# Linear attention and gated feed-forward: banks, order and sums of the attention's first pairs

## The chip, the cores and the metric

The kernel runs on one core of a Trainium2 chip, in one launch. Its time is the device time in microseconds; the median of three runs counts. The core's engines are TensorE (PE in the profile, with its weight loads as PEld), VectorE (DVE), ScalarE (ACT), GpSimd (POOL) and SyncE (SP), which issues all DMAs here. Each engine works off its own instructions strictly in the order of the program, and semaphores make it wait for the others.

## What is computed

First an attention with feature maps, for 8 batches and 8 heads of 576 x 64; its output, 4608 tokens of 512 features, then goes through a gated feed-forward layer.

```python
def phi(x):
    proj = np.einsum('bhsd,df->bhsf', x, w_phi)
    proj = proj - np.max(np.abs(proj), axis=-1, keepdims=True)
    return np.concatenate([np.exp(proj), np.exp(-proj)], axis=-1)
q_p, k_p = (phi(q), phi(k))
kv = np.einsum('bhsf,bhsd->bhfd', k_p, v)
z = np.sum(k_p, axis=2)
num = np.einsum('bhsf,bhfd->bhsd', q_p, kv)
den = np.einsum('bhsf,bhf->bhs', q_p, z)[..., None] + 1e-06
x = (num / den)                       # to (4608, 512)
gate = 1.0 / (1.0 + np.exp(-(x @ w_gate)))
out = gate * (x @ w_val) @ w_out      # d_model 512, d_ff 1536
```

## The kernel before

The attention works on pairs of heads: 32 steps, numbered 0 to 31, four to a batch (NP = 4). A pair i passes through these steps, each a function of the listing:

- `load`, `load_v`: K, Q and V from DRAM into buffers of which there are two each.
- `keys` and `rest`: the projections of K on TensorE, in three parts (`pk_0`, `pk_1` in `k_heads`, `pk_2` in `rest`). `k_exp` then takes the maximum (`mx`, L432) and the difference (`dk`, L445) on VectorE, and both exponentials (`ek`, L454) on ScalarE. From pair EARLY on, `k_sum` adds up four blocks of the exponentials per head on VectorE (`s2`, `su`, L467 and L468).
- `q_half`: a half of Q's projection on TensorE for each head (`pq`, L411); `copies` brings it to `d` on ScalarE (L473). `q_max` finds the maximum over the features on VectorE (L500 to L513: a transposing reduction `pm`, small copies to `pn`, a transpose to `mb`) and subtracts it from `d` (L518). `q_exp` makes both exponentials on ScalarE, `eq0` and `eq1` (L564), into one buffer each; `d` has two buffers.
- `kv`: the products of the key exponentials with V, and their sums over the sequence by products with ones (`kvz`, L528 and L542): five blocks per head, or two where `k_sum` has added four. `turn` transposes the result (`tp`, L554); ScalarE copies before and behind it (`kvt`, `kv`).
- `num`: numerators `nm` (L580) and denominators `dp` (L591) on TensorE, copied by ScalarE to `ex` (L597) and `dr` (L607). `norm` brings the denominators through DRAM to every row (three DMAs: `dn`, `den`, `rb`), takes the reciprocal, and `scale` multiplies (`xp`, L634) and stores x. For the last pair of the first batch (`soon=True`) the denominators are computed for every row instead, without the DMAs. In the first batch `scale` also splits x into `xh` and `xl` in place, for the feed-forward's first chunks.

PSUM is cut into pools: `ps_gv` (two banks, gate and value products), `ps_a` (five banks, everything of the attention, through the helper `bank`), and `ps_acc` (one bank, output products).

While the attention runs, `half_units` gives the work of the feed-forward's first four blocks of d_ff on chunks of 256 tokens: half units of twelve gate or value products (`gv`, L164), the gating on ScalarE and VectorE (`gate`), and outputs of twelve products (`acc`, L171). `fill` puts half units between the attention's steps at a given rate; `queue` makes a batch's chunks due LAG spots later. `weigh` makes the twelve weight tiles of these blocks (`weight_tile`: three cheap and two longer VectorE instructions and one of ScalarE, L133 to L143) as far as `grant` allows. Generators in `tasks` go on by one step at each `tick`; where a tick stands sets where their instructions come in the engines' queues. The rest of the feed-forward (L171 and L164 on tiles of 512 tokens) follows from about 700 us on.

The order is written by hand: one loop for pairs -1 to EARLY - 1 = 3 (L728 to L752), then `num` of pair 3 with `soon`, then one loop from pair EARLY - 1 on (L756 to L784) with `fill` in it.

Of the kernel before, what the change touches and what calls it, by code (L numbers as in the profile page):

```python
# [20 lines left out]
F = 128  # L21
# [15 lines left out]
EARLY = NP  # L37
RATE = 2.8
LAG = (2, 8)
# [5 lines left out]
def attention_moe(  # L45
# [306 lines left out]
    with ExitStack() as actx:  # L352
# [9 lines left out]
        def bank(shape, name):  # L362
            return ps_a.tile(shape, F32, tag="a", name=name)
# [14 lines left out]
        steps = [(b, p) for b in range(B) for p in range(NP)]  # L378
# [23 lines left out]
        def q_half(i, hf):  # L402

            n = f"{i}_{hf}"
            if hf == 0:
                ds[i] = at.tile([P, 2, S], F32, tag="d", name=f"d{i}")
            x, d = loaded["q", i], ds[i]
            cs = slice(hf * HS, hf * HS + HS)
            pps = [bank([P, HS], f"pq{n}{hd}") for hd in range(2)]
            for hd in range(2):  # L410
                nc.tensor.matmul(  # L411
                    pps[hd], wk[head(hd), :], x[head(hd), cs], start=True, stop=True
                )
            return [(d[:, hd, cs], pps[hd]) for hd in range(2)]
# [64 lines left out]
        def rest(i):  # L479
            kx = loaded.pop(("k", i))  # L480
            pp = bank([P, 4, F], f"pk{i}_2")
            nc.tensor.matmul(pp[:, 0, :], kx[:, 4 * P :], wk, start=True, stop=True)  # L482
# [37 lines left out]
        def kv(i):  # L520
# [3 lines left out]
            kvz = bank([P, 3 * F], f"kvz{i}")  # L524
# [25 lines left out]
        def turn(i):  # L550
            kvt = kvs[i]
            tp = bank([P, 3, P], f"tp{i}")
# [5 lines left out]
        def q_exp(i):  # L558
            yield
            d = ds.pop(i)  # L560
            es = []
            for sg in range(2):
                e = at.tile([P, 2, S], F32, tag=f"eq{sg}", name=f"eq{i}_{sg}", bufs=1)
                act.activation(e, d, AF.Exp, scale=1.0 - 2.0 * sg)  # L564
                es.append(e)
                yield
            exps[i] = es

        def num(i, soon=False):
# [4 lines left out]
            nms = [bank([P, HS], f"nm{i}_{hf}") for hf in range(2)]  # L574
            dps = [bank([P, HS], f"dp{i}_{hf}") for hf in range(1 + soon)]
            for hf in range(2):
                cs = slice(hf * HS, hf * HS + HS)
                for sg in range(2):
                    for o in range(0, P, Q):
# [4 lines left out]
                        )  # L584
            for n, dp in enumerate(dps):
# [10 lines left out]
            for hf in range(2):  # L596
                act.copy(ex[:, hf * HS : hf * HS + HS], nms[hf])  # L597
# [12 lines left out]
        def norm(i, ex, dr):  # L610
# [4 lines left out]
            for _ in range(3):  # L615
                yield
# [10 lines left out]
            for _ in range(4):  # L627
                yield
            yield from scale(i, ex, rb)

        def scale(i, ex, rb):
# [3 lines left out]
            for c in range(S // CH if b == 0 else 0):  # L635
# [3 lines left out]
                ps = slice(p * CH, p * CH + CH)  # L639
                split(xs[c][0][:, ps], xs[c][1][:, ps], xp[:, c * CH : c * CH + CH])  # L640
                parts[c] += 1
            yield
# [79 lines left out]
        N = len(steps)  # L722
# [5 lines left out]
        for i in range(-1, EARLY):  # L728
            load(i + 2 if i >= 0 else N)
            if i + 1 < EARLY:  # L730
                keys(i + 1)
                copies(q_half(i + 1, 0))
                tick()
                tick()
                copies(q_half(i + 1, 1))
                rest(i + 1)
                start(q_max(i + 1))
                tick()
# [11 lines left out]
            tick()  # L750
            tick()
            grant(i)  # L752
        num(EARLY - 1, True)
        grant(6)
        queue(0)
        for i in range(EARLY - 1, N + 1):  # L756
            if EARLY <= i:
                load(i + 2)
                grant(3 * (i - 1))
# [8 lines left out]
            if i < EARLY:  # L768
                fill()
                fill()  # L770
                continue
# [94 lines left out]
```

## Time and profile before

| | us |
|---|---|
| three runs | 1295.61, 1295.95, 1300.03 |
| median | 1295.95 |
| the profiled execution | 1297.41 |
| its span, first to last instruction | 1295.6 |
| TensorE busy in it | 1228.6 (95%) |
| VectorE busy | 797.9 (62%) |
| ScalarE busy | 526.8 (41%) |
| mean granted TensorE clock | 0.97 |

The page's slices cut the span into 40 equal parts of 32 us; a digit is the busy share in tenths, and PEclk the granted TensorE clock in tenths:

```profile
PE   7848899999999999999889999999999999999998
DVE  6699888788878778883894953424343434333333
PEclk8967899999999999999899999999999999999999
```

Engines overlap, so busy shares do not add up to the span; a stage is read by the engine that is full in it and by what the others wait for.

### The profile page before, as it was taken

What the parts mean: (1) busy time and instruction counts of PE and PEld (TensorE: products, weight loads), DVE (VectorE), ACT (ScalarE), POOL (GpSimd) and SP (SyncE); (2) the same over time, 40 slices, a digit from 0 to 9 for tenths busy, and PEclk for the clock granted to TensorE, in tenths of its full rate; (3) what the DMA queues carried; (4) which work ended last, traced back from release to release, by engine and by line L of the source; (5) the groups of instructions that cost most, each with busy time, mean ns of one, the idle gap of its engine ahead of it and who ended that gap; (6) DMA issues with size and microseconds to landing.
All of it is one profiled execution on the core that took longest, in us unless ns stands there. A gap on an engine that the chain in (4) does not pass through costs nothing.

```text
span 1295.6 us, 22470 instructions
## 1 busy us (share of the span) xinstructions
PE 1228.6 (95%) x9120; PEld 970.1 (75%) x9120; DVE 797.9 (62%) x1608; ACT 526.8 (41%) x1081; POOL 0.7 (0%) x6
## 2 busy tenths in 40 slices
PE   7848899999999999999889999999999999999998
PEld 5535566777777777777778888888888888888886
DVE  6699888788878778883894953424343434333333
ACT  4535556665565566564443422222222222222221
POOL 0000000000000000000000000000000000000000
PEclk8967899999999999999899999999999999999999
DMA  4556344343343334332763620202011111111010
GB/s 175 178 178 243 105 124 136 98 137 97 124 127 111 110 104 126 105 109 72 264 209 133 209 98 1 83 15 71 28 58 40 57 42 46 52 39 60 5 61 33
DMA packets 80868, 131.55 MB, mean 102 GB/s; under 512 B 18300, under 2 KB 37884, under 8 KB 80764
## 3 DMA queue, kind: packets, MB, share of 16 engines
q1 hardware_dynamic: 80764, 130.11, 30.9%
q8 instruction: 72, 1.18, 0.4%
q14 instruction: 32, 0.26, 0.1%
HBM read 92.04 MB, written 28.45 MB: 93 GB/s over the span
## 4 chain that ended last, share of the span: by engine, by line
PE 81%; DVE 11%; ACT 3%; issue 2%; DMA 2%; SPq 0%; DVEq 0%; ACTq 0%
PE acc L171 21%; PE g L164 15%; PE v L164 15%; PE gv L164 12%; PE kvz L528 5%; PE nm L580 4%; PE pq L411 2%; PE dp L591 2%; PE pk L421 2%; ACT eq L564 1%; PE kvz L542 1%; DMA wraw<-w_moe 1%; PE pk L482 1%; DVE mb L513 1%; PE tp L554 1%
## 5 line engine op out<-in xcount | busy, mean ns | idle before, releaser
L164 PE MATMUL gv<-xh,wh 128*128 128x256 f32 x576 | 174.5, 303 | 17.0 <-ACT xh L62 11.9
L171 PE MATMUL acc<-wh,hh 128*128 128x512 f32 x432 | 172.4, 399 | 3.4 <-ACT hh L234 2.7
L164 PE MATMUL gv<-xl,wh 128*128 128x256 f32 x576 | 167.2, 290 | 2.8 <-DVE xl L211 2.8
L171 PE MATMUL acc<-wh,hl 128*128 128x512 f32 x432 | 169.2, 392 | 0.7 <-DVE hl L236 0.7
L171 PE MATMUL acc<-wl,hh 128*128 128x512 f32 x432 | 169.1, 392 | 0.0
L164 PE MATMUL gv<-xh,wl 128*128 128x256 f32 x576 | 166.5, 289 | 0.0
L164 PEld LDWEIGHTS gv<-xh,wh 128*128 128x128 f32 x576 | 114.1, 198 | 34.6 <-issue 14.9
L62 ACT CAST hh<-u 128x512 fp32r<-128x512 f32 x72 | 44.7, 621 | 229.4 <-DVE u L185 229.4
L183 DVE TENSOR_SCALAR t<-t 128x512 uint32<-128x512 uint32 x72 | 30.7, 426 | 167.2 <-ACT t L180 167.2
L164 PEld LDWEIGHTS gv<-xl,wh 128*128 128x128 f32 x576 | 114.1, 198 | 3.9 <-DVE xl L211 3.0
L180 ACT ACTIVATE t<-g 128x512 f32<-128x512 f32 x72 | 43.0, 598 | 179.5 <-PE g L164 179.3
L164 PEld LDWEIGHTS gv<-xh,wl 128*128 128x128 f32 x576 | 114.0, 198 | 0.0
L164 PE MATMUL g<-xh,wh 128*128 128x512 f32 x288 | 113.0, 392 | 0.0
L164 PE MATMUL v<-xh,wh 128*128 128x512 f32 x288 | 112.6, 391 | 0.0
L164 PE MATMUL g<-xh,wl 128*128 128x512 f32 x288 | 112.5, 391 | 0.0
L164 PE MATMUL g<-xl,wh 128*128 128x512 f32 x288 | 112.5, 391 | 0.0
L164 PE MATMUL v<-xl,wh 128*128 128x512 f32 x288 | 112.3, 390 | 0.0
L164 PE MATMUL v<-xh,wl 128*128 128x512 f32 x288 | 112.1, 389 | 0.0
L184 DVE SCALAR_TENSOR_TENSOR t<-t,v 128x512 f32<-128x512 f32 x72 | 49.4, 686 | 97.7 <-PE v L164 97.7
L171 PEld LDWEIGHTS acc<-wh,hh 128*128 128x128 f32 x432 | 81.1, 188 | 26.2 <-issue 4.8
L171 PEld LDWEIGHTS acc<-wh,hl 128*128 128x128 f32 x432 | 81.2, 188 | 20.2 <-DVE hl L236 1.7
L171 PEld LDWEIGHTS acc<-wl,hh 128*128 128x128 f32 x432 | 81.3, 188 | 15.8
(92 smaller groups left out, 2120.5 us busy)
## 6 DMA issues: line engine op xcount, KB each, us to landing
wraw<-w_moe SPq DMA_DIRECT2D x36, 512.0 KB, 4.6
xl<-xs SPq DMA_DIRECT2D x34, 512.0 KB, 3.9
k<-k SPq DMA_DIRECT2D x32, 320.0 KB, 3.7
v<-v SPq DMA_DIRECT2D x32, 320.0 KB, 2.9
q<-q SPq DMA_DIRECT2D x32, 288.0 KB, 4.1
wh<-wtop SPq DMA_DIRECT2D x36, 256.0 KB, 2.3
ys<-y SPq DMA_DIRECT2D x36, 256.0 KB, 2.0
yp<-ys SPq DMA_DIRECT2D x36, 256.0 KB
```

The costliest lines, as they stand in the source:

```text
L62: a = act.copy(h, x)
L164: nc.tensor.matmul(o, a[:, ws], x[:, cs], start=i == 0, stop=i == 11)
L171: nc.tensor.matmul(acc, a[:, ts], w[:, ws], start=first and i == 0, stop=last and i == 2)
L180: act.activation(t, g, AF.Tanh, scale=0.5)
L183: vec.tensor_scalar(tu, tu, 0x7FFFFFFF, None, op0=ALU.bitwise_and)
L184: vec.scalar_tensor_tensor(t, t, 1.0, vl, op0=ALU.add, op1=ALU.mult)
L411: nc.tensor.matmul(pps[hd], wk[head(hd), :], x[head(hd), cs], start=True, stop=True)
L421: nc.tensor.matmul(pps[hd][:, t, :], kx[head(hd), t * P : t * P + P], wk[head(hd), :], start=True, stop=True,)
L482: nc.tensor.matmul(pp[:, 0, :], kx[:, 4 * P :], wk, start=True, stop=True)
L528: nc.tensor.matmul(kvz[o : o + Q, : 2 * F], vx[:, 2 * t + hd, o % D : o % D + Q], (e0, e1)[hd][:, t, :] if t < 4 else e2[:, 0, :], start=t ...
L580: nc.tensor.matmul(nms[hf][o : o + Q, :], w[:, sg, o : o + Q], es[sg][:, o // D, cs], start=sg == 0, stop=sg == 1, tile_position=(0, o),)
L591: nc.tensor.matmul(dp[o : o + Q, :], w[:, 2, z : z + Q], es[sg][:, hd, hf * HS : hf * HS + HS], start=sg == 0, stop=sg == 1, tile_position ...
```

## The change

Six things change in the first 200 us:

- In the first batch (pairs 0 to 3) the KV products and their transposes use the output bank (`ps_acc`), numerators and denominators the two gate and value banks (`ps_gv`), since the feed-forward has not begun. `bank` chooses by the pair's number. `ps_a` then holds only the projections.
- `num` copies the numerators to `ex` ahead of the denominators' products (which then need only the bank of the first).
- Q's second exponential is written over `d`, which gets a third buffer; the first has two buffers under one name (`eq`).
- The sums of the keys stay on TensorE up to pair 9 (ONPE = 10), where VectorE added up blocks from pair 4 on: pairs 4 to 9 get twelve more products with ones and lose four VectorE additions each.
- The order in the first batch is written anew: `rest` (`pk_2`) comes behind `kv`, the `norm` of the first batch waits fewer ticks, and pair 4 is projected in the loop's last round, ahead of pair 3's numerators. `scale` makes all copies `xh`, then yields, then all differences `xl`.
- The feed-forward's queue starts behind that loop, with LAG 4 instead of 2 (the old second loop began one round earlier), and the weight tiles 3 to 5 are granted only there.

```diff
+ONPE = 10
-LAG = (2, 8)
+LAG = (4, 8)
...
-        def bank(shape, name):
+        def bank(shape, name, i=N, ps=None, tag=None):
+
+            if i < EARLY:
+                return ps.tile(shape, F32, tag=tag, name=name)
             return ps_a.tile(shape, F32, tag="a", name=name)
...
-                ds[i] = at.tile([P, 2, S], F32, tag="d", name=f"d{i}")
+                ds[i] = at.tile([P, 2, S], F32, tag="d", name=f"d{i}", bufs=3)
...
-                if i >= EARLY:
+                if i >= ONPE:
                     yield
                     yield from k_sum(i)
...
-            kvz = bank([P, 3 * F], f"kvz{i}")
+            kvz = bank([P, 3 * F], f"kvz{i}", i, ps_acc, "acc")
...
-            tp = bank([P, 3, P], f"tp{i}")
+            tp = bank([P, 3, P], f"tp{i}", i, ps_acc, "acc")
...
-            es = []
-            for sg in range(2):
-                e = at.tile([P, 2, S], F32, tag=f"eq{sg}", name=f"eq{i}_{sg}", bufs=1)
-                act.activation(e, d, AF.Exp, scale=1.0 - 2.0 * sg)
-                es.append(e)
-                yield
-            exps[i] = es
+            e = at.tile([P, 2, S], F32, tag="eq", name=f"eq{i}")
+            act.activation(e, d, AF.Exp)
+            yield
+            act.activation(d, d, AF.Exp, scale=-1.0)
+            exps[i] = e, d
+            yield
...
-            nms = [bank([P, HS], f"nm{i}_{hf}") for hf in range(2)]
-            dps = [bank([P, HS], f"dp{i}_{hf}") for hf in range(1 + soon)]
+            nms = [bank([P, HS], f"nm{i}_{hf}", i, ps_gv, "gv") for hf in range(2)]
             for hf in range(2):
...
+                act.copy(ex[:, cs], nms[hf])
+            dps = [bank([P, HS], f"dp{i}_{hf}", i, ps_gv, "gv") for hf in range(1 + soon)]
...
-            for _ in range(3):
+            for _ in range(3 if i >= EARLY else 2):
                 yield
...
-            for _ in range(4):
+            for _ in range(4 if i >= EARLY else 2):
                 yield
...
         for i in range(-1, EARLY):
             load(i + 2 if i >= 0 else N)
...
+            if i == EARLY - 1:
+                start(q_exp(i))
+            keys(i + 1)
+            copies(q_half(i + 1, 0))
+            copies(q_half(i + 1, 1))
+            if i == EARLY - 1:
                 tick()
             if i >= 0:
                 kv(i)
-                start(q_exp(i))
+            tick()
+            rest(i + 1)
             if i >= 1:
                 num(i - 1)
             tick()
+            start(q_max(i + 1))
+            if 0 <= i < EARLY - 1:
+                start(q_exp(i))
             tick()
             if i >= 0:
                 turn(i)
                 load_v(i + 2)
-            tick()
-            tick()
+            if i == EARLY - 1:
+                num(i, True)
+            for _ in range(3):
+                tick()
             grant(i)
-        num(EARLY - 1, True)
-        grant(6)
         queue(0)
-        for i in range(EARLY - 1, N + 1):
-            if EARLY <= i:
-                load(i + 2)
-                grant(3 * (i - 1))
+        for i in range(EARLY, N + 1):
+            load(i + 2)
+            grant(3 * (i - 1))
```

What this does to the queues, at three places. TensorE, at the end of pair 2's projections (`pq2`, `pk2`; `kvz1` are pair 1's KV products, `nm0` and `dp0` pair 0's numerators and denominators). Before:

```order
L411 MATMUL pq2_10_400<-q0_2_250,wk_134 128x288
L411 MATMUL pq2_11_401<-q0_2_250,wk_134 128x288
L482 MATMUL pk2_2_406<-wk_134,k0_2_248 128x128
L528 MATMUL kvz1_429<-ek1_0_264,v0_1_178 32x256 x2
L528 MATMUL kvz1_429<-ek1_1_267,v0_1_178 32x256 x2
```

Now, behind all of pair 1's KV products:

```order
L548 MATMUL kvz1_399<-ek1_2_332,halves_130 32x128 x4
L488 MATMUL pk2_2_446<-wk_134,k0_2_248 128x128
L584 MATMUL nm0_0_452<-eq0_345,kv0_351 32x288 x4
L584 MATMUL nm0_0_452<-d0_204,kv0_351 32x288 x4
L584 MATMUL nm0_1_453<-eq0_345,kv0_351 32x288 x4
```

The last key projection of pair 2 moved from ahead of the 40 rows of `kvz1` to behind them; the second operand of the numerators is now `d0`.

VectorE, with the same pair's maxima (`mx2`, `dk2` of the keys, `pm2`, `pn2` of Q) and pair 0's reloaded denominators (`dn0`). Before:

```order
L432 TENSOR_REDUCE mx2_2_408<-pk2_2_406 128x1
L445 TENSOR_TENSOR dk2_2_413<-pk2_2_406,mx2_2_408 128x128
L500 TENSOR_REDUCE pm2_415<-d2_387 128x36
L505 COPY pn2_416<-pm2_415 64x36
L506 COPY pn2_416<-pm2_415 64x36
L507 TENSOR_TENSOR pm2_415<-pm2_415,pn2_416 128x36
L510 COPY pn2_416<-pm2_415 32x36 x4
L511 TENSOR_TENSOR pm2_415<-pm2_415,pn2_416 128x36
L513 STREAM_TRANSPOSE mb2_417<-pm2_415 128x1152
L518 TENSOR_TENSOR d2_387<-d2_387,mb2_417 128x1152
L617 TENSOR_SCALAR dn0_504<-dn0_504 128x9
L618 RECIPROCAL dn0_504<-dn0_504 128x9
```

Now:

```order
L438 TENSOR_REDUCE mx2_2_448<-pk2_2_446 128x1
L451 TENSOR_TENSOR dk2_2_487<-pk2_2_446,mx2_2_448 128x128
L506 TENSOR_REDUCE pm2_494<-d2_386 128x36
L621 TENSOR_SCALAR dn0_483<-dn0_483 128x9
L622 RECIPROCAL dn0_483<-dn0_483 128x9
L511 COPY pn2_495<-pm2_494 64x36
```

The reloaded denominators moved from behind pair 2's subtraction (`d2`) to ahead of its small copies.

VectorE, around pair 4's subtraction (`d4`; `xl1_1` the split of x, `s2_4` and `su4` pair 4's sums, `wtop`, `wmid`, `wl` weight tiles). Before:

```order
L63 TENSOR_TENSOR xl1_1_701<-xp2_974,xh1_1_700 128x256
L467 TENSOR_TENSOR s2_4_980<-ek4_0_882 128x512
L468 TENSOR_TENSOR su4_981<-s2_4_980 128x256
L518 TENSOR_TENSOR d4_886<-d4_886,mb4_949 128x1152
L137 SCALAR_TENSOR_TENSOR wtop1_1_970<-wraw1_1_911,wtop1_1_970 128x512
L467 TENSOR_TENSOR s2_4_980<-ek4_1_885 128x512
L468 TENSOR_TENSOR su4_981<-s2_4_980 128x256
```

Now, with pair 3's outputs (`rb3`, `xp3`) ahead of it:

```order
L606 TENSOR_SCALAR rb3_912<-dp3_0_894 128x288
L607 RECIPROCAL rb3_912<-rb3_912 128x288
L606 TENSOR_SCALAR rb3_912<-dp3_1_895 128x288
L607 RECIPROCAL rb3_912<-rb3_912 128x288
L638 TENSOR_TENSOR xp3_917<-ex3_873,rb3_912 128x576
L621 TENSOR_SCALAR dn2_837<-dn2_837 128x9
```
```order
L649 TENSOR_TENSOR xl1_0_665<-xp3_917,xh1_0_664 128x256
L649 TENSOR_TENSOR xl1_1_668<-xp3_917,xh1_1_667 128x256
L519 STREAM_TRANSPOSE mb4_863<-pm4_861 128x1152
L524 TENSOR_TENSOR d4_727<-d4_727,mb4_863 128x1152
L438 TENSOR_REDUCE mx5_0_953<-pk5_0_943 128x4
```

Pair 4's sums are gone, the work of pair 3's outputs moved to between its maxima and its subtraction, and pair 2's outputs (`xp2`) and the weight tiles of block 1 moved behind it.

More of the change, by code (lines that the diff above doesn't have):

```diff
@@ L360, in attention_moe @@
         ps_acc = actx.enter_context(tc.tile_pool(name="ps_o", bufs=1, space=PSUM))
-        def bank(shape, name):
+        steps = [(b, p) for b in range(B) for p in range(NP)]
+        N = len(steps)
+        def bank(shape, name, i=N, ps=None, tag=None):
+            if i < EARLY:
+                return ps.tile(shape, F32, tag=tag, name=name)
             return ps_a.tile(shape, F32, tag="a", name=name)
@@ L377, in attention_moe @@
         ]
-        steps = [(b, p) for b in range(B) for p in range(NP)]
         loaded, ks, ds, exps, kvs, rbs = {}, {}, {}, {}, {}, {}
@@ L595, in num @@
                         )
-            for hf in range(2):
-                act.copy(ex[:, hf * HS : hf * HS + HS], nms[hf])
             if soon:
@@ L638, in scale @@
                     xs[c] = x_tiles(moe, CH, f"1_{c}")[:2]
-                ps = slice(p * CH, p * CH + CH)
-                split(xs[c][0][:, ps], xs[c][1][:, ps], xp[:, c * CH : c * CH + CH])
+                act.copy(
+                    xs[c][0][:, p * CH : p * CH + CH], xp[:, c * CH : c * CH + CH]
+                )
+            yield
+            for c in range(S // CH if b == 0 else 0):
+                xh, xl = (x[:, p * CH : p * CH + CH] for x in xs[c])
+                vec.tensor_tensor(
+                    xl, xp[:, c * CH : c * CH + CH], xh.bitcast(F32), op=ALU.subtract
+                )
                 parts[c] += 1
-            yield
             t = 0
@@ L720, in grant @@
                 wdone += 1
-        N = len(steps)
         for i in range(2):
@@ L729, in attention_moe @@
             load(i + 2 if i >= 0 else N)
-            if i + 1 < EARLY:
-                keys(i + 1)
-                copies(q_half(i + 1, 0))
-                tick()
-                tick()
[L735 to L738, printed above, removed]
+            if i == EARLY - 1:
[4 more added lines that the diff above has]
+            if i == EARLY - 1:
                 tick()
@@ L749, in attention_moe @@
                 load_v(i + 2)
-            tick()
-            tick()
+            if i == EARLY - 1:
+                num(i, True)
+            for _ in range(3):
+                tick()
             grant(i)
-        num(EARLY - 1, True)
-        grant(6)
         queue(0)
-        for i in range(EARLY - 1, N + 1):
-            if EARLY <= i:
-                load(i + 2)
-                grant(3 * (i - 1))
+        for i in range(EARLY, N + 1):
+            load(i + 2)
+            grant(3 * (i - 1))
             if i + 1 < N:
@@ L767, in attention_moe @@
                 fill()
[L768 to L771, printed above, removed]
             if i < N:
```

## The prediction

> **What bounds the kernel now.** I read three views in this order: the page's busy shares in slices, the table of windows by stage, and the timeline of TensorE (PE), VectorE (DVE) and ScalarE (ACT) where that table shows idle time. Four windows (columns: window, its length, then busy us of PE, weight loads, DVE, ACT, GpSimd, the granted TensorE clock, the share of DMA, GB/s):
>
> ```profile
> 0.00:60.00 60.00, 45.94 (x596) 30.32 (x600) 41.33 (x92) 34.01 (x70) 0.70 (x6) 0.91 0.49 167
> 60.00:140.00 80.00, 51.45 (x433) 36.03 (x422) 71.72 (x150) 34.73 (x77) 0.00 (x0) 0.72 0.62 207
> 140.00:200.00 60.00, 54.80 (x642) 37.93 (x641) 51.78 (x111) 36.75 (x82) 0.00 (x0) 0.97 0.38 109
> 200.00:580.00 380.00, 379.24 (x4114) 289.80 (x4115) 308.51 (x683) 227.05 (x517) 0.00 (x0) 1.00 0.38 116
> ```
>
> From 200 us on TensorE is the bound: 379.24 of 380 us busy. Before that it idles 14.1 + 28.6 + 5.2 = 47.8 us, and between 60 and 140 us its clock falls to 0.72, because VectorE is full there (71.72 of 80 us). The change touches only what stands before about 200 us: in the program's order, from pair 18 on, TensorE has the same rows in the same order. So what the change wins or loses is the time at which TensorE enters its full stretch, and that shift should reach the end undiminished. The marker I use is the last Q projection of pair 11, at 199.18 us:
>
> ```profile
> 18.12 4.50 PE L528 MATMUL kvz<-ek,v 128*32 128x256 f32 x40 [3.63 <-issue]
> 59.09 2.15 PE L580 MATMUL nm<-eq,kv 128*32 128x288 f32 x32 [3.18 <-ACT kv L556]
> 136.05 1.32 PE L411 MATMUL pq<-q,wk 64*128 64x288 f32 x2 [4.99 <-ACT d L473]
> 152.80 0.84 PE L411 MATMUL pq<-q,wk 64*128 64x288 f32 x2 [1.44 <-ACT d L473]
> 199.18 0.75 PE L411 MATMUL pq<-q,wk 64*128 64x288 f32 x2 [2.28 <-ACT d L473]
> ```
>
> Most of TensorE's waits end with ScalarE copying a Q half out of a bank (d, L473), and that copy stands in ScalarE's queue behind work that VectorE delivers late. The marker is a good one, because by that instruction both orders have issued the same eight units of gate and value products and the same two output products.
>
> **The ten sums.** Pairs 4 to 9 lose four VectorE instructions each and get twelve small products more. The groups of the sums, and on the timeline the ones products of an early pair (16 of them) beside those of pair 10's kind (4):
>
> ```profile
> L467 DVE TENSOR_TENSOR s<-ek 128x512 f32<-128x512 f32 x56 | 37.6, 671 | 0.0
> L468 DVE TENSOR_TENSOR su<-s 128x256 f32<-128x256 f32 x56 | 23.8, 425 | 1.9
> 51.25 1.06 PE L542 MATMUL kvz<-ek,ones 128*32 128x128 f32 x32
> 52.12 0.40 PE L542 MATMUL kvz<-ek,halves 128*32 128x128 f32 x8
> ```
> ```profile
> 164.43 1.16 PE L421 MATMUL pk<-wk,k 64*128 64x128 f32 x16
> 165.43 0.65 PE L411 MATMUL pq<-q,wk 64*128 64x288 f32 x4
> ...
> 167.63 0.76 PE L411 MATMUL pq<-q,wk 64*128 64x288 f32 x4
> 168.31 0.49 PE L482 MATMUL pk<-wk,k 128*128 128x128 f32 x2
> ...
> 170.16 2.37 PE L528 MATMUL kvz<-ek,v 128*32 128x256 f32 x40
> 172.34 0.40 PE L542 MATMUL kvz<-su,ones 128*32 128x128 f32 x8
> 172.56 0.40 PE L542 MATMUL kvz<-ek,halves 128*32 128x128 f32 x8
> 172.78 2.12 PE L580 MATMUL nm<-eq,kv 128*32 128x288 f32 x32
> 174.72 1.15 PE L591 MATMUL dp<-eq,kv 128*32 128x288 f32 x16
> 175.80 0.38 PE L164 MATMUL gv<-xh,wh 128*128 128x256 f32 x1
> ```
>
> VectorE gives up 2 x 0.671 + 2 x 0.425 = 2.19 us a pair, 13.2 us in six pairs. TensorE pays from start to start 52.12 - 51.25 = 0.87 instead of 172.56 - 172.34 = 0.22 us, so 0.65 a pair and 4 us in all, before 200 us. Up to pair 7 that lies in its idle time; for pairs 8 and 9 it does not.
>
> **Banks of the first batch, and pair 4 ahead of the last numerators.** The bank wait of 3.63 us at 18.12 goes: the first KV product can follow pair 1's Q projection at about 14 us. But each pair's last key projection (pk_2) now stands behind the KV product, the maxima that VectorE takes of it wait there, and the denominators' reload (dn) stands in VectorE's queue one step earlier, ahead of the small copies.
>
> ```profile
> 28.74 2.37 PE L528 MATMUL kvz<-ek,v 128*32 128x256 f32 x40
> 40.60 4.05 PE L528 MATMUL kvz<-ek,v 128*32 128x256 f32 x40 [1.02 <-issue]
> ```
> ```profile
> 37.67 0.17 DVE L617 TENSOR_SCALAR dn<-dn 128x9 f32<-128x9 f32 x1 [1.61 <-DMA dn<-dr]
> 62.27 0.46 DVE L602 TENSOR_SCALAR rb<-dp 128x288 f32<-128x288 f32 x1 [3.46 <-PE dp L591]
> 86.51 1.35 DVE L518 TENSOR_TENSOR d<-d,mb 128x1152 f32<-128x1152 f32 x1
> 110.66 1.35 DVE L518 TENSOR_TENSOR d<-d,mb 128x1152 f32<-128x1152 f32 x1
> 146.81 1.35 DVE L518 TENSOR_TENSOR d<-d,mb 128x1152 f32<-128x1152 f32 x1
> ```
> ```profile
> 35.18 0.40 ACT L607 COPY dr<-dp 128x288 f32<-128x288 f32 x1 [0.57 <-PE dp L591]
> ```
> ```profile
> L454 ACT ACTIVATE ek<-dk 128x512 f32<-128x512 f32 (+1 forms) x192 | 87.5, 520 | 11.9 <-DVE dk L445 11.5
> L564 ACT ACTIVATE eq<-d 128x1152 f32<-128x1152 f32 x64 | 71.7, 1164 | 0.0
> ```
>
> I walked the new order through the first batch with these rows. One pair is a loop: the last Q half goes when ScalarE has copied the first; then the KV product, cold, since TensorE has idled some 4 us (4.05 + about 0.9 for the ones and halves = 4.9, where 28.74 shows 2.37 warm); pk_2 0.25; numerators and denominators 3.0; ScalarE's copies behind them about 1.2; the next key exponentials, 6 x 0.52 = 3.1; the two Q exponentials and the KV copy, 2.8; and a copy. That is 15.2 to 15.8 us: the last Q half of pairs 2, 3 and 4 at about 24, 39 and 55 us. VectorE waits in each: about 2.4 us for pair 2's pk_2, then 3.6 for dn (35.18 + 0.40 to 37.67 is 2.1 us of DMA, and the copy comes at 33.4), then 1 to 3.4 for later ones. The wait of 3.46 at 62.27 stays as one of 3.4, now after pair 4's maxima. Behind dn on VectorE's queue stand the small copies, the transpose and the subtraction of the same pair, and the next pair's maxima; ScalarE's exponentials wait for them. The walk ends with pair 4's subtraction done at 82 us, where it was 86.51 + 1.35 = 87.9. The estimate may be off by 4 us either way: three cold KV products found warm would give 5 back, a DMA 2 us slower twice would take 4.
>
> On SyncE the loads of pair 6's K and Q and one reload now stand behind the stores of pair 3's outputs, at 77 us; they are needed from about 88 us on, so some 4 us cover them. GpSimd's queue holds six instructions, all in the first window, and nothing is moved past it.
>
> **Feed-forward later, weights later (LAG and grants).** From pair 4 to pair 5 the old order took 24.15 us on VectorE (110.66 - 86.51), nearly without waits. It held about 3.7 weight tiles, 2.2 us of sums and two gates; the new one holds 2.3 tiles, no gate, no sum, and pair 2's scaling.
>
> ```profile
> L133 DVE TENSOR_SCALAR wtop<-wraw 128x512 uint32<-128x512 uint32 x12 | 4.9, 409 | 0.0
> L137 DVE SCALAR_TENSOR_TENSOR wtop<-wraw,wtop 128x512 uint32<-128x512 uint32 x12 | 8.2, 680 | 3.4 <-ACT wtop L134 3.4
> L231 DVE SCALAR_TENSOR_TENSOR t<-t,gv 128x256 f32<-128x256 f32 x72 | 30.3, 421 | 8.1
> ```
>
> A tile is three instructions like the first and two like the second, 2.6 us; a gate is three like the third, 1.3. So 1.4 x 2.6 + 2.2 + 2.6 - 0.75 = 7.7 us less: pair 5 done at 98.5 instead of 112.0. The tiles come back with pairs 6 and 7: 3.5 tiles more (9.1), two pairs' sums less (4.4), so 40.8 us for the two where 36.15 stand now (146.81 - 110.66): pair 7 at about 139 instead of 148.2. Here the lead is 9 us, and VectorE stops being the bound.
>
> For then TensorE has its bill to pay. By pair 8's projections the old order had done 5.5 units of gate and value products, the new one 3.5. From pair 8's last Q half to the marker the new order has, by the block above and these pieces of the chain,
>
> ```profile
> 218.29 1.44 PE gv L164 x12
> 219.73 2.75 PE acc L171 x12
> ```
>
> three KV products at 2.62 + 0.65, three times 3.02 and pk_2, tp, pk and the two pq at about 0.25 + 0.3 + 1.0 + 1.2, eight half units at 1.5 and two outputs at 2.9: 9.8 + 9.1 + 8 + 12 + 5.8 = 45 us. It starts at about 143.5 (the old one at 152.80), and I add 5 us for one wait for a Q copy and two cold KV products: marker at 193.5 instead of 199.2. The old kernel then runs cold for another 1.5 us, the new one, which comes to the marker without a stall, mostly not. With half of that the shift is 6 us.
>
> **The second exponential in place** costs nothing: the same instruction, 1164 ns, and a third d buffer in place of the second eq. The numerators read d three pairs before the buffer is written again. If that cover were gone, the Q copies would wait for numerators of the pair before, at most 3 us a pair. The copies of the numerators ahead of the denominators' bank cost 0 to 0.4 us a pair in the first batch and are in the loop.
>
> **The sum.** The profiled execution took 1297.41 us, its span 1295.6. Minus 6 it is 1291.4. The median of the three runs, 1295.95, lies 1.5 lower, which gives 1290.
>
> **A rule on the clock.** The row at 40.60 shows a KV product at 4.05 us after a wait of only 1.02, that at 59.09 numerators at full pace after 3.18. The Trainium skill ("TensorE: Matmul & The Clock Gate", section "What's actually happening") lets the clock fall after an idle window of about 3.4 us and come back after as long a busy one. By that rule the first batch's gaps of 4 us cost what I count, but the short wait at pair 9 would cost nothing and the sum would be 1.7 us lower; the trace at 40.60 speaks against it, that at 59.09 for it.
>
> **The rivals.** (1) *All of VectorE's relief arrives.* TensorE stays warm in the first batch (5 us) and the 9 us lead of pair 7 lasts to the marker: about 13 us, 1283. For it: the 13.2 us of sums, the cold stretches are counted in full. Against: 45 us of TensorE work from pair 8. (2) *The lead is given back.* The deferred units and the 4 us of ones products meet waits of 2 us more in each of pairs 9 to 11; the marker stands where it stood: 1296. For it: the waits for Q copies at 136.05, 152.80 and 199.18, all with VectorE under full load. (3) *Slower, by one mechanism:* at pairs 9 to 11 the copy of the first Q half stands in ScalarE's queue behind a gate's cast that needs VectorE, and each pair stalls as at 136.05, 4.99 us and a cold start of 1.7: 143.5 + 45 + 3 x 6.7 = 208.6, 9 us late, 1305. It decides from 3.7 us a pair on, (199.2 - 143.5 - 45) / 3. (4) *Nothing moves*, because the full stretch waits for a load or a store instead: 1296.
>
> **How the numbers follow.** Forecast 0.50 (1286 to 1294, half of it below 1289.5), rival 1 0.17, rival 2 0.22, rival 3 0.09, rival 4 0.02. A measurement of this kernel can tell about 0.5% from no change, 6.5 us: faster 0.25 + 0.17 = 0.42, same 0.25 + 0.22 + 0.02 = 0.49, slower 0.09. The range takes in rivals 1, 2 and 4 and leaves out rival 3 and the far end of 1: 1281 to 1298.
>
> **What would show it.** Right: VectorE idle some 2 to 4 us per pair between 28 and 72 us, at pk_2, dn and dp; pair 4's subtraction near 82, pair 7's near 139 us; TensorE without long waits from about 160 us; the marker near 193.5; 4 us more of ones products. Wrong: a marker past 199, Q copies that make TensorE wait over 3 us at pairs 9 to 11, or idle time of TensorE after 200 us that was not there before.

## The result, and the profile after

The changed kernel took 1290.78 us in the median of 12 runs (1288.41 to 1295.23); the kernel before took 1297.60 us beside it (1295.61 to 1301.52). The ratio is 0.9949, with a 95% interval of 0.9934 to 0.9963. A second series of the same two kernels gave 1293.10 against 1299.40 us, a ratio of 0.9958 (0.9942 to 0.9974). Neither interval reaches 1, so there is a gain; it lies between 0.26 and 0.66% by the two together, about the 0.5% that the prediction took for the least that can be told. The profiled execution took 1293.53 us with a span of 1291.7, 3.9 us less than the 1297.41 and 1295.6 of before. It is one of the slower ones of its kernel, so the trace shows less of a gain than the medians do.

The table of windows of the changed kernel (columns as in the prediction):

```profile
0.00:60.00 60.00, 45.45 (x501) 27.74 (x505) 41.73 (x92) 32.28 (x68) 0.70 (x6) 0.87 0.47 160
60.00:140.00 80.00, 58.34 (x679) 37.88 (x672) 66.42 (x142) 38.47 (x84) 0.00 (x0) 0.80 0.66 217
140.00:200.00 60.00, 56.95 (x642) 41.42 (x641) 45.60 (x99) 35.57 (x78) 0.00 (x0) 0.94 0.36 106
200.00:580.00 380.00, 380.00 (x4128) 291.12 (x4126) 311.45 (x688) 229.89 (x522) 0.00 (x0) 1.00 0.38 116
```

VectorE has 66.42 us of work in the second window instead of 71.72. TensorE idles 14.6 + 21.7 + 3.1 = 39.3 us before 200 us instead of 47.8, and not at all from there to 580 us. Some 4 us of what was idle (six pairs at 0.65) now hold the ones products.

VectorE's timeline of the changed kernel: the waits that the prediction named, and the subtraction of the maximum (d) of pairs 2 to 5, 7 and 9:

```profile
31.45 0.29 DVE L438 TENSOR_REDUCE mx<-pk 128x1 f32<-128x128 f32 x1 [3.98 <-PE pk L488]
37.04 0.17 DVE L621 TENSOR_SCALAR dn<-dn 128x9 f32<-128x9 f32 x1 [3.61 <-DMA dn<-dr]
40.54 1.36 DVE L524 TENSOR_TENSOR d<-d,mb 128x1152 f32<-128x1152 f32 x1
55.48 1.36 DVE L524 TENSOR_TENSOR d<-d,mb 128x1152 f32<-128x1152 f32 x1
72.80 0.46 DVE L606 TENSOR_SCALAR rb<-dp 128x288 f32<-128x288 f32 x1 [3.27 <-PE dp L597]
82.35 1.36 DVE L524 TENSOR_TENSOR d<-d,mb 128x1152 f32<-128x1152 f32 x1
98.15 1.35 DVE L524 TENSOR_TENSOR d<-d,mb 128x1152 f32<-128x1152 f32 x1
...
140.85 1.36 DVE L524 TENSOR_TENSOR d<-d,mb 128x1152 f32<-128x1152 f32 x1
...
174.00 1.36 DVE L524 TENSOR_TENSOR d<-d,mb 128x1152 f32<-128x1152 f32 x1
```

And TensorE's timeline, from pair 6's second Q half to the KV product of pair 11. The marker, the last Q projection of pair 11, is now in the row at 197.62, which holds both heads of the half (the second starts some 0.35 us into it); the last key projection (pk_2) right behind it is easier to compare:

```profile
104.98 1.33 PE L417 MATMUL pq<-q,wk 64*128 64x288 f32 x2 [5.16 <-ACT d L479]
125.71 1.13 PE L417 MATMUL pq<-q,wk 64*128 64x288 f32 x2 [2.35 <-ACT d L479]
...
146.54 1.29 PE L417 MATMUL pq<-q,wk 64*128 64x288 f32 x2 [1.50 <-DVE dk L451]
...
197.62 1.09 PE L417 MATMUL pq<-q,wk 64*128 64x288 f32 x4
198.64 0.49 PE L488 MATMUL pk<-wk,k 128*128 128x128 f32 x2
...
201.92 2.37 PE L534 MATMUL kvz<-ek,v 128*32 128x256 f32 x40
...
321.39 0.49 PE L488 MATMUL pk<-wk,k 128*128 128x128 f32 x2
```

The same place in the kernel before, which adds pk_2 of pair 11, what follows, and pk_2 of pair 18 to the row at 199.18 in the prediction:

```profile
199.86 0.49 PE L482 MATMUL pk<-wk,k 128*128 128x128 f32 x2
...
200.90 0.28 PE L164 MATMUL gv<-xh,wh 128*128 128x256 f32 x1
201.15 0.41 PE L164 MATMUL gv<-xh,wl 128*128 128x256 f32 x1
...
202.13 3.52 PE L528 MATMUL kvz<-ek,v 128*32 128x256 f32 x40
...
325.19 0.49 PE L482 MATMUL pk<-wk,k 128*128 128x128 f32 x2
```

At pk_2 of pair 11 the changed kernel leads by 199.86 - 198.64 = 1.2 us, and at the end by 3.9. The rest comes behind the marker: the lead is 325.19 - 321.39 = 3.8 us at pk_2 of pair 18. The kernel before had waited 2.28 us at the marker, and some 2 us later its products slow down from 0.28 to 0.41 us, and its KV product takes 3.52 us where the changed kernel's takes 2.37. The windows between the two pk_2, of before and then of the changed kernel, and two windows of before around the place where its products slow down:

```profile
199.86:325.19 125.33, 124.57 (x1353) 93.88 (x1352) 102.04 (x225) 75.24 (x171) 0.00 (x0) 0.99 0.39 120
198.64:321.39 122.75, 122.75 (x1352) 93.20 (x1351) 102.69 (x226) 76.13 (x172) 0.00 (x0) 1.00 0.40 120
```
```profile
197.80:201.10 3.30, 1.92 (x12) 1.53 (x13) 2.74 (x6) 3.27 (x7) 0.00 (x0) 1.00 0.76 207
201.20:204.50 3.30, 3.30 (x29) 1.90 (x32) 2.26 (x4) 1.37 (x5) 0.00 (x0) 0.50 0.31 102
```

The changed kernel comes through without idle time and at the full clock. The kernel before idles 125.33 - 124.57 = 0.76 us and has a granted clock of 0.50 in the window of 3.3 us from 201.2 on, which costs some 1.7 us (an estimate: half of it). Together that is nearly all of the 2.6 us by which it is longer.

### The profile page after: what moved, and what is told of

Same layout as the page of the kernel before. It is cut to its first block, busy times and chain, and to the rows that moved or that the text cites. A ratio compares the mean times of both kernels' runs of the same rounds, so it can differ in the third digit from the quotient of the medians.

```text
span 1291.7 us, 22705 instructions
## 1 busy us (share of the span) xinstructions
PE 1234.4 (96%) x9264; PEld 971.2 (75%) x9264; DVE 786.1 (61%) x1584; ACT 528.1 (41%) x1081; POOL 0.7 (0%) x6
## 4 chain that ended last, share of the span: by engine, by line
PE 86%; DVE 7%; DMA 3%; ACT 2%; issue 1%; SPq 0%; DVEq 0%
PE acc L172 22%; PE g L165 15%; PE v L165 15%; PE gv L165 13%; PE kvz L534 6%; PE nm L584 4%; PE pq L417 3%; PE dp L597 2%; PE pk L427 2%; PE kvz L548 1%; DMA wraw<-w_moe 1%; PE pk L488 1%; ACT ek L460 1%; PE tp L560 1%; DMA rb<-den 1%
## 5 line engine op out<-in xcount | busy, mean ns | idle before, releaser
L165 PE MATMUL gv<-xh,wh 128*128 128x256 f32 x576 | 171.6, 298 | 4.9 <-ACT xh L210 2.6
L165 PE MATMUL gv<-xl,wh 128*128 128x256 f32 x576 | 164.5, 286 | 2.8 <-DVE xl L212 2.8
L165 PEld LDWEIGHTS gv<-xh,wh 128*128 128x128 f32 x576 | 111.5, 194 | 22.7 <-issue 15.7
L534 PE MATMUL kvz<-ek,v 128*32 128x256 f32 x1280 | 89.6, 433 | 6.8 <-issue 5.8
```

Of the source, the lines that this page charges most:

```text
L165: nc.tensor.matmul(o, a[:, ws], x[:, cs], start=i == 0, stop=i == 11)
L534: nc.tensor.matmul(kvz[o : o + Q, : 2 * F], vx[:, 2 * t + hd, o % D : o % D + Q], (e0, e1)[hd][:, t, :] if t < 4 else e2[:, 0, :], start=t ...
```

## The experiments

**1. The sums, undone and alone.** The changed kernel with the sums of pairs 4 to 9 back on VectorE (`a_sums_dve`; the text speaks of ten sums, since pairs 0 to 3 have theirs on TensorE in both kernels, but six pairs' sums are moved):

```diff
-ONPE = 10
+ONPE = 4
```

> The changed kernel with one thing undone: the ten sums of pairs 4 to 9 are on VectorE again. Theory (the gain is VectorE's relief between 80 and 140 us, and TensorE's longer bill then eats most of it): pairs 4 to 7 get 4 x 2.2 = 8.8 us of VectorE work back, so pair 7's subtraction of the maximum starts at about 149 to 150 us instead of 140.85, later than the 146.81 of the kernel before; the marker (last Q projection of pair 11) stands at 200 to 203 us instead of 197.62, and the time is 3 to 5 us above the changed kernel's, near 1295. Rival (the new order of the first batch and its banks make the gain, the sums only trade VectorE time for TensorE time): pair 7 later by 8 us, but the marker within 1 us of 197.62 and the time within 1 us of 1290.8, since TensorE saves 4 us of ones products.

The kernel before with the sums of these six pairs alone on TensorE (`b_sums_pe`):

```diff
 EARLY = NP
+ONPE = 10
...
-                if i >= EARLY:
+                if i >= ONPE:
```

> The kernel before with the ten sums alone moved to TensorE (pairs 4 to 9). Theory: pair 7's subtraction starts at about 138 us instead of 146.81 (8.8 us of VectorE work gone, nearly all of it on the path), the marker moves from 199.18 to about 196 to 198, and the time falls by 2 to 4 us to about 1294. Rival (the sums only trade): the marker stays within 1 us of 199.18 and the time within 1 us of 1297.6.

Measured: without the sums 1300.68 us, ratio to before 1.0018 (1.0008 to 1.0029); with the sums alone 1290.19 us, ratio 0.9939 (0.9926 to 0.9953). **The sums alone bring as much as the whole change, and the rest of the change without them makes the kernel a little slower.** Both theories were right in their direction, and their sizes were too small: 7.9 us for 2 to 4, and 9.9 for 3 to 5. Pair 7 came out near what was expected (148.35 us without the sums, 141.00 with them alone, for 149 to 150 and 138); the marker moved further than expected (205.54 for 200 to 203, and 193.32 for 196 to 198). VectorE's timeline of the kernel with the sums alone shows the subtraction of pairs 4, 5, 7 and 9:

```profile
85.08 1.35 DVE L519 TENSOR_TENSOR d<-d,mb 128x1152 f32<-128x1152 f32 x1
108.54 1.35 DVE L519 TENSOR_TENSOR d<-d,mb 128x1152 f32<-128x1152 f32 x1
...
141.00 1.36 DVE L519 TENSOR_TENSOR d<-d,mb 128x1152 f32<-128x1152 f32 x1
...
171.63 1.36 DVE L519 TENSOR_TENSOR d<-d,mb 128x1152 f32<-128x1152 f32 x1
```

TensorE's timeline of the same kernel, with a wait of 8.41 us that the kernel before has too, and the marker:

```profile
84.42 0.58 PE L165 MATMUL gv<-xh,wh 128*128 128x256 f32 x1 [8.41 <-ACT xh L63]
...
193.32 0.91 PE L412 MATMUL pq<-q,wk 64*128 64x288 f32 x2 [2.28 <-ACT d L474]
194.16 0.80 PE L483 MATMUL pk<-wk,k 128*128 128x128 f32 x2
```

Pair 4 leads by 1.4 us against the kernel before (86.51), pair 7 by 5.8 (146.81), and pk_2 of pair 11 by 199.86 - 194.16 = 5.7: the lead of pair 7 arrives undiminished. The changed kernel reaches pair 7 at the same time (140.85), though it was 10 us ahead at pair 5 (98.15 against 108.54), and then falls behind: 174.00 against 171.63 at pair 9, 198.64 against 194.16 at pk_2 of pair 11. Most of that is work put off: up to pair 8's pk_2 it has issued 96 gate and value products, the other 132, and by pair 11 both have 192. The 36 products are three half units, 4.3 us at the 1.44 us that one takes in the prediction's block. Behind pair 11 it gets some back: from there to pk_2 of pair 18 it takes 122.8 us, the kernel with the sums alone 125.1, with a wait and a stretch at half clock like the kernel before. Without the sums (TensorE's timeline of `a_sums_dve`) the same pk_2 stands 6.4 us later than in the kernel before:

```profile
206.22 0.49 PE L488 MATMUL pk<-wk,k 128*128 128x128 f32 x2
```

**2. Where the sums stop paying.** The kernel before with the sums of all pairs from 4 to 31 on TensorE (`b_sums_all`, ONPE = 32).

> The kernel before with the sums of all pairs from 4 to 31 on TensorE instead of those of pairs 4 to 9: 22 pairs more, 48 us less on VectorE, 22 x 0.65 = 14.3 us more on TensorE. Theory (relief of VectorE counts only while VectorE sets the pace, up to about 200 us; behind it TensorE is the bound and pays the full 0.65 us a pair): the marker stays at 193 to 195 us (193.32 with ten sums), TensorE idles no less behind it, and the time is 12 to 15 us above 1290.2, near 1304. Rival (VectorE's load also slows the later stretch, through waits that TensorE's busy share hides): the time is 0 to 8 us above 1290.2.

Measured: 1303.19 us, 13.0 above the 1290.19 of ten sums, so 13.0 / 22 = 0.59 us a pair; ratio to before 1.0039 (1.0025 to 1.0052). The window from 200 to 580 us of this kernel:

```profile
200.00:580.00 380.00, 379.91 (x4415) 294.76 (x4411) 262.29 (x578) 224.31 (x505) 0.00 (x0) 1.00 0.38 113
```

VectorE has 262.29 us of work there instead of 308.51, TensorE has no less than before, and the relief buys nothing. This is the theory, at the price that the rows of before gave (0.65 us a pair).

**3. The feed-forward's start.** The changed kernel with LAG 2 (`a_lag2`), and the kernel with the sums alone with LAG 6 (`b_sums_lag6`):

```diff
-LAG = (4, 8)
+LAG = (2, 8)
```

> The changed kernel with the gate and value products of the first chunk started two places earlier again (LAG 2 instead of 4). Theory (deferring them is neutral: VectorE is spared between 82 and 98 us, TensorE pays later): pair 5's subtraction starts some 2 to 4 us after the 98.15 us of the changed kernel, TensorE has less to make up at pairs 8 to 10, and the time is within 2 us of 1290.8. Rival 1 (the deferral is what makes pair 5 early and with it the gain): pair 7 at 146 us or later, the marker at 199 or later, the time at 1294 to 1297. Rival 2 (the deferral gives the lead back): the marker at 195 or earlier for the same work issued ahead of it, and the time at 1287 to 1289.

> The kernel before with the ten sums on TensorE, and LAG 6 instead of 2: the first gate and value products stand behind pair 5's projections instead of ahead of them. In the kernel with the sums alone TensorE waits 8.41 us at 84.42 for the split of the feed-forward's input, with pair 5's projections queued behind. Theory (such a head-of-line wait at LAG 2 is why the changed kernel with LAG 2 lost 7.5 us, and VectorE's gates are better placed later): pair 5's subtraction starts at 99 to 103 us instead of 108.54, pair 7's at 137 to 141 instead of 141.00, and the time is 0 to 4 us under 1290.2. Rival (the deferred products are owed and come due at pairs 8 to 11): pair 5 early all the same, the marker at 193 to 197 where it is 193.32, the time 0 to 4 us above 1290.2.

Measured: the changed kernel with LAG 2 took 1298.33 us (ratio 1.0003, 0.9987 to 1.0020), 7.5 more than with LAG 4. That is rival 1 by the marker (199.84) and by the time, which is even longer than it gave, but not by its reason: pair 5's subtraction starts at 98.14 us as with LAG 4 (98.15), and the loss begins at pair 6 (121.51 instead of 118.58). In the profile 1.9 us are lost up to pk_2 of pair 11, and 2.7 behind it, where TensorE again waits and runs at half clock (125.5 us to pair 18 instead of 122.8). The sums alone with LAG 6 took 1289.60 us (0.9939, 0.9926 to 0.9952), the same as with LAG 2: neither a gain nor a loss. Pair 5 is earlier (105.29 instead of 108.54, where 99 to 103 were expected), and the lead is gone at the marker (194.31 instead of 193.32), as the rival had it. TensorE's timeline of the changed kernel with LAG 2 shows a wait for the split of the feed-forward's input, with pair 4's KV product queued behind it, at 91.85 us instead of 86.28:

```profile
89.72 0.58 PE L165 MATMUL gv<-xh,wh 128*128 128x256 f32 x1 [6.91 <-ACT xh L643]
...
200.52 0.49 PE L488 MATMUL pk<-wk,k 128*128 128x128 f32 x2
```

The last piece of that input is ready later in the changed kernel. ScalarE's timeline of the changed kernel, and then of the kernel with the sums alone:

```profile
89.27 0.71 ACT L643 CAST xh<-xp 128x256 fp32r<-128x256 f32 x2 [1.90 <-DVE xp L638]
```
```profile
83.96 0.71 ACT L63 CAST xh<-xp 128x256 fp32r<-128x256 f32 x2 [0.28 <-DVE xp L635]
```

The last piece is pair 2's output (xp2) in both. In the new order it stands on VectorE behind pair 4's subtraction (82.35 us) and pair 5's first maxima, and is scaled at 88.48 us; with the sums alone it stands ahead of pair 4's subtraction (85.08) and is scaled at 83.17. So the input is complete 5.3 us later, and LAG 4 reads as what the new order needs, not as a gain in itself. In the old order the later start only changes one wait of TensorE for another. The timeline of `b_sums_lag6` has, in place of the 8.41 us, a wait for a Q copy that stands on ScalarE behind a weight tile's step, which waits for VectorE:

```profile
88.74 1.32 PE L412 MATMUL pq<-q,wk 64*128 64x288 f32 x2 [10.97 <-ACT d L474]
```

**4. The banks.** The changed kernel with the first batch's banks shared again (`a_banks_back`), and the sums alone with the KV product and its transposes in the output product's bank (`b_sums_kvbank`):

```diff
-            if i < EARLY:
+            if i < 0:
                 return ps.tile(shape, F32, tag=tag, name=name)
```

> The changed kernel with the first batch's KV, transposes, numerators and denominators back in the five shared PSUM banks. Theory (the banks only spare the first batch's bank wait, 3.63 us at 18.12 us before; VectorE and ScalarE bound the stretch behind it): pair 4's subtraction starts 0 to 4 us later than 82.35, the marker is 0 to 2 us later than 197.62 and the time 0 to 2 us above 1290.8. Rival (the banks are what makes the gain): pair 4 at 86 us or later, the marker at 199 or later, the time at 1295 or more.

> The kernel before with the ten sums on TensorE, and the KV product and the transposes of the first batch in the output product's bank. Theory (the wait of 3.66 us for a bank at 18.07 is the only one that the shared banks cost, and VectorE sets what follows): TensorE's KV product of pair 0 starts at 14 to 15 us, the first Q half of pair 2 at 22 to 24 instead of 26.07, pair 4's subtraction 1 to 3.5 us before 85.08, the time 0 to 3 us under 1290.2. Rival (the time saved at 18 us is waited for again at the next load or copy): pair 4's subtraction within 0.7 us of 85.08, time within 1 us of 1290.2.

Measured: 1293.07 us (0.9953, 0.9935 to 0.9970) and 1291.16 us (0.9941, 0.9926 to 0.9956). In the first, pair 4's subtraction is 2 us late (84.33), as the theory had it, but its interval lies over that of the changed kernel, so the 2.3 us between the medians are not shown to be a loss. In the second the wait of 3.66 us at 18.07 is gone, and TensorE waits 5.03 us for the copy of the KV product a little later (its timeline):

```profile
21.59 0.88 PE L557 MATMUL tp<-ident,kvt 128*128 128x128 f32 x3 [5.03 <-ACT kvt L550]
```

Pair 4's subtraction is at 84.91 instead of 85.08: the rival.

**5. The two waits of VectorE in the first batch.** In the changed kernel, pk_2 ahead of the KV product again (`a_pk2_first`):

```diff
+            rest(i + 1)
             if i >= 0:
                 kv(i)
             tick()
-            rest(i + 1)
```

the denominators later again (`a_norm_ticks`):

```diff
-            for _ in range(3 if i >= EARLY else 2):
+            for _ in range(3):
...
-            for _ in range(4 if i >= EARLY else 2):
+            for _ in range(4):
```

and both (`a_both`).

> The changed kernel with one order undone: in the first batch's loop each pair's last key projection (pk_2) is issued ahead of the KV product again. Theory (the new order of the first batch costs what it wins, since VectorE waits at pk_2: 3.98 us at 31.45, 1.49 at 46.45, 2.45 at 62.95): these waits go, pair 3's subtraction starts at 50 to 53 us instead of 55.48 and pair 4's 2 to 4 us before 82.35; TensorE and ScalarE pass on about half, marker and time 1 to 3 us earlier than the changed kernel's. Rival (the wait only moves to the reload of the denominators, 3.61 us at 37.04, and to the ScalarE copies behind it): pair 4's subtraction within 1 us of 82.35, the time within 1 us of 1290.8.

> The changed kernel with the denominators of pairs 0 to 3 (dn, then the product with them) put into VectorE's queue one and two ticks later again. Theory (VectorE's wait of 3.61 us for the DMA at 37.04 holds up the transpose, the subtraction and the next maxima): the wait is under 1 us, pair 2's subtraction starts 2 to 3.6 us before 40.54, pair 4's 1 to 3 us before 82.35, time 0 to 2 us less. Rival (the scaling that then comes later stands ahead of pair 4's or 5's projections and delays the feed-forward's first input): pair 4 within 1 us, pair 5 later by 1 to 3 us, the time 0 to 3 us above 1290.8.

> The changed kernel with both orders of the first batch undone at once: pk_2 ahead of the KV product, and the denominators one and two ticks later. Alone, the first left VectorE waiting 7.82 us for the denominators' DMA at 37.82, the second left it waiting 2.4 to 3.3 us for pk_2. Theory (VectorE's two waits lie beside each other, so that only both together give anything): pair 2's subtraction at 29 to 33 us (40.54), pair 3's at 46 to 50 (55.48), pair 4's at 76 to 79 (82.35), the time 1 to 4 us under the changed kernel's. Rival (ScalarE's copies and exponentials set the pace of the loop, 15 us a pair, whatever VectorE waits for): pair 2's subtraction earlier, but pair 4's at 80 to 82 and the time within 1 us.

Measured: 1294.37 us (0.9976, 0.9962 to 0.9989), 1291.17 us (0.9948, 0.9933 to 0.9963) and 1293.47 us (0.9962, 0.9948 to 0.9977). None is faster than the changed kernel. With pk_2 ahead the median is 3.6 us longer than that of the changed kernel's first series, but only 1.3 longer than that of its second (experiment 7, 0.9942 to 0.9974), and in its profile the subtractions from the first pair to pair 9 lie 0.8 to 2 us later, 1.06 of it from the start; so a loss is not shown for certain. With the denominators later, pair 4's subtraction is 2 us earlier, 0.95 of it from the start, as its theory had it, but the median shows no gain. `a_both` ran beside the second series and is level with it. VectorE's timelines of the three kernels in turn show the waits that took the place of those removed:

```profile
37.82 0.17 DVE L621 TENSOR_SCALAR dn<-dn 128x9 f32<-128x9 f32 x1 [7.82 <-DMA dn<-dr]
...
83.35 1.36 DVE L524 TENSOR_TENSOR d<-d,mb 128x1152 f32<-128x1152 f32 x1
```
```profile
69.63 0.46 DVE L606 TENSOR_SCALAR rb<-dp 128x288 f32<-128x288 f32 x1 [6.37 <-PE dp L597]
...
80.33 1.35 DVE L524 TENSOR_TENSOR d<-d,mb 128x1152 f32<-128x1152 f32 x1
```
```profile
73.97 0.46 DVE L606 TENSOR_SCALAR rb<-dp 128x288 f32<-128x288 f32 x1 [10.00 <-PE dp L597]
...
84.67 1.35 DVE L524 TENSOR_TENSOR d<-d,mb 128x1152 f32<-128x1152 f32 x1
```

With both orders undone VectorE waits 10 us in one place, and pair 4 comes no earlier (84.67 us, where the rival gave 80 to 82). So up to 75 us VectorE is not what sets the pace of the new order. That ScalarE's copies and exponentials set it, as the rival says, fits but is not shown: TensorE still waits for Q copies there (3.18, 3.23 and 4.42 us at 24.11, 39.03 and 56.71 in `a_both`), 15 and 18 us apart; the loop of the prediction was 15.2 to 15.8.

**6. The exponential in place.** The kernel before with that edit alone (`b_inplace`):

```diff
-            for sg in range(2):
-                e = at.tile([P, 2, S], F32, tag=f"eq{sg}", name=f"eq{i}_{sg}", bufs=1)
-                act.activation(e, d, AF.Exp, scale=1.0 - 2.0 * sg)
+            e = at.tile([P, 2, S], F32, tag="eq", name=f"eq{i}")
+            act.activation(e, d, AF.Exp)
+            act.activation(d, d, AF.Exp, scale=-1.0)
```

> The kernel before with Q's second exponential in place alone (a third buffer for d, one tag of two for eq). Theory (same instruction, no new wait): all marks of the trace within 0.7 us of the kernel before, the time within 1.5 us of 1297.6. Rival (the buffers of eq, free a pair earlier, let ScalarE's exponentials start ahead of the numerators): ScalarE's waits for numerators go and the marker is 1 us or more early.

Measured: 1300.02 us, ratio 1.0014 (1.0003 to 1.0025): neither. Up to pair 7 its marks lie within 0.3 us of the kernel before. Then one KV product is slow; TensorE's timeline of the kernel before, and of this one:

```profile
140.21 2.37 PE L528 MATMUL kvz<-ek,v 128*32 128x256 f32 x40
```
```profile
140.36 3.40 PE L528 MATMUL kvz<-ek,v 128*32 128x256 f32 x40
```

It stands behind nearly the same waits (4.99 and 5.16 us). The granted clock differs: two windows of the kernel before, and one of this one:

```profile
132.90:139.60 6.70, 3.55 (x12) 2.80 (x13) 5.44 (x14) 2.61 (x7) 0.00 (x0) 0.50 0.73 222
139.70:142.50 2.80, 2.80 (x49) 1.81 (x52) 1.70 (x2) 1.47 (x5) 0.00 (x0) 1.00 0.00 0
```
```profile
135.80:142.50 6.70, 6.68 (x37) 4.55 (x40) 4.95 (x9) 3.45 (x9) 0.00 (x0) 0.50 0.43 134
```

In both executions the clock is at half for some 6.7 us; in the kernel before that ends just ahead of the KV product, here behind it. From here this execution runs about 1 us behind, from pair 11 on 3. So the slow product is the moment of the clock's change. Whether the edit moves that moment, or each execution has another, one profile does not tell; the median says that the edit costs about 2 us by itself, and why is open.

**7. The changed kernel again** (`after_again`).

> The changed kernel once more, for a second profile beside the same runs of before as the two kernels below. Theory (executions of one kernel differ by a start some 1 us earlier or later and by a few short waits that leave TensorE's clock low or not, 2 to 3 us in all): marks within 1.5 us of the first profile up to pair 7 (140.85), the marker between 194 and 199, ratio to before 0.993 to 0.997. Rival (the marks are the same in every execution, and the spread arises after 200 us): marker within 0.5 us of 197.62.

Measured: 1293.10 us, ratio 0.9958 (0.9942 to 0.9974); profiled at 1294.65. Pair 4's subtraction is at 82.44 (82.35 in the first profile), pair 7's at 142.19 (140.85), pk_2 of pair 11 at 199.81 (198.64). The two profiles differ by 1.2 us at the end, and all of it is there at the marker, so the theory holds for these two; where the larger spread of the runs (1288.41 to 1295.23) arises is not shown. That the changed kernel leads little or not at all at the marker (1.2 us in one profile, 0.05 in the other) is no accident of one execution.

## Why the prediction came out

The forecast was 1290.0 us, and the median came to 1290.78, within the range given. The chances stood on both sides of the limit of 0.5%, and so do the two ratios, 0.9949 and 0.9958. That the number is so close is in part luck. The sum took 6 us off the profiled execution, nearly all of them up to the marker, where two profiles show 1.2 and 0.05 us; the work behind the marker brought more than was given, the rest of the median's gain is not seen in the profiles, and the median of before, from three runs 1295.95, came to 1297.60 beside the changed kernel. The account of what causes the gain was incomplete.

- **The bound** was right. From 200 us on TensorE is busy for all of 380 us, the order is unchanged, and relieving VectorE behind that point buys nothing (experiment 2).
- **The first batch** was right in its times and its waits, up to 1.7 us: the last Q halves of pairs 2, 3 and 4 stand at 23.59, 40.23 and 55.84 (24, 39 and 55 were given), the waits at pk_2, dn and dp are 3.98, 3.61 and 3.27 us (2.4, 3.6 and 3.4), and pair 4's subtraction is done at 83.7 us (82).
- **Pair 5** is done at 99.5 us (98.5). But this lead of 12.5 us is worth little, as the kernel with the sums alone shows: 10 us behind at that point, it is level at pair 7.
- **Pair 7 and the marker are the step that failed.** Pair 7 was to be done at 139 us and the marker to stand at 193.5. They stand at 142.2 and 197.62. Of the 4.1 us, 3.0 are there at pair 8's second Q half (146.54, where 143.5 was given). The walk was right that VectorE sets the pace of pairs 6 and 7, but sized its work too small: from pair 5's subtraction to pair 7's it takes 42.7 us, where 40.8 were given, and pair 5 was already 1.0 us late. Eight weight tiles are finished there against four before; by their instructions' times they cost 10.6 us more, where 3.5 tiles (9.1 us) were counted. VectorE also waits 2.9 us in all, 0.7 more than before, mostly for DMAs. TensorE's waits of 5.16 us at 104.98 and 2.35 at 125.71 come from this: the Q copies stand on ScalarE behind its step of a weight tile, which waits for VectorE. From pair 8 to the marker it takes 51.1 us, where 45 + 5 were given; that bill was sized well. So rival 2, the lead given back, was nearer the trace at the marker than the forecast, but through pairs 6 and 7 rather than 9 to 11, where TensorE waits 0.84 us in all. In the second profile the marker's row is at 198.54, close to the 199 that was named as a sign of being wrong.
- **What followed the marker was worth more than given.** Half of a cold stretch of 1.5 us was counted; it measured 2.6 us, 0.76 of idle time and the rest at half clock. From pk_2 of pair 11 to that of pair 18 both kernels issue the same products; the kernel before takes 325.19 - 199.86 = 125.3 us for them and the changed one 321.39 - 198.64 = 122.8. With the 1.2 us at the marker that makes 3.8 of the 3.9 us of the profiled executions. The median's gain of 6.8 is larger than that of either profiled pair (3.9 and, in the second series, 1295.6 - 1292.9 = 2.7); this part can't be traced.
- **The ten sums** were sized rightly on each engine (0.65 us a pair given, 0.59 measured; page and windows show VectorE relieved by 797.9 - 786.1 = 11.8 us), but the text did not say what they are worth alone. Alone they bring as much as the whole change: 5.7 us at the marker and 7.9 us in the median. The other parts together add nothing to it that could be measured: with them 4.5 us less of the lead is there at the marker, and 2.3 us more is won behind it. The prediction added pair 4's lead, the deferral and the sums up along one path; the runs show that the deferral is needed where the new order delays the feed-forward's input, and gains nothing where it doesn't (experiment 3). The later grant of the weight tiles was not undone by itself.
- **The exponential in place** was put at nothing. By itself it cost 2.3 us in the medians, an interval of 0.4 to 3.2 by the ratio; its part in the changed kernel was not measured. The new order needs this edit or another buffer, since pair 3's exponentials are issued ahead of pair 2's numerators and would have to wait for them in a single buffer; the changed kernel without it was not tried.
- **The slower rival** did not occur: TensorE waits 1.50 us at pair 8's Q halves and less behind them, under the 3.7 us a pair from which it decides (its own quotient, (199.2 - 143.5 - 45) / 3, is 3.6).

No variant beats the changed kernel for certain. The sums alone, and the two variants of them, took 1289.6 to 1291.2 us at ratios of 0.9939 to 0.9941; the changed kernel's two series gave 0.9949 and 0.9958, and the intervals overlap. One edit of two lines, the sums, does as well as the whole change.

## What to carry to other kernels

An early lead on one engine's milestones is worth only what is left of it where the bounding engine fills up; compare the two traces there, at a place by which both have issued the same work, and not at the first place where they part. A bundle of edits is best taken apart: move work off the saturated engine alone first, and only as far as the bounding engine has idle time to take it. Where a wait is removed and nothing happens, look for the wait that grew in its place: here 5.03 us stood for 3.66, and 10.97 for 8.41.

## What the runs showed of the hardware

TensorE's clock did not follow the waits at once, nor in the same way each time. In the kernel before, a wait of 2.28 us ended at 199.18, the products still ran at 0.28 us at 200.90 and at 0.41 only from 201.15 on; the KV product behind them took 3.52 us. In the kernel with the sums alone the same wait of 2.28 us is followed by slower projections at once (0.91 and 0.80 us at 193.32 and 194.16, where 199.18 and 199.86 show 0.75 and 0.49). And the KV product at 140 us took 2.37 us in one kernel and 3.40 in another behind nearly equal waits. So a wait of 2.28 us costs the KV product behind it between nothing and 1.2 us here, by when the stretch at half clock falls: the granted clock is 0.50 from about 201.1 to 204.5 us in the kernel before, over the KV product at 202.13, and from about 193.8 to 197.2 with the sums alone, where the KV product starts at 197.36. The Trainium skill ("TensorE: Matmul & The Clock Gate", section "What's actually happening") has the clock judged in free-running windows, which agrees with this scatter; its idle window of about 3.4 us is longer than the 2.28 us that sufficed here.
